# New orders for the opening and for steps 18 to 46, earlier row weights for expert 0, activations moved by 64 bytes, and a last tile in two column halves

## The chip, the core and the metric

The kernel runs as one program on one core of a Trainium2 chip. A core has TensorE (PE, whose weight loads the profile lists apart as PEld), VectorE (DVE), ScalarE (ACT), GpSimd (POOL) and SyncE (SP, which here only issues DMAs). The metric is the device time of one execution in microseconds (us), lower is better.

## The reference, cut to what matters

```python
# attention: 4 batches, 8 heads, 576 positions, 64 wide; banded masks (plain for 4 heads, dilated for 4)
scores = scale * np.matmul(q, k.transpose(0, 1, 3, 2))
scores = np.where(masks, scores, -1e9)
attn = softmax(scores)
x = np.matmul(attn, v)                      # -> 2304 tokens x 512
# dense block, d_ff = 2048
h = x @ w_in
x = (h * np.cos(h)) @ w_out
# 8 experts, two per token, d_ff = 1024
noisy = x @ w_gate + np.log1p(np.exp(x @ w_noise)) * noise
# the two largest of each token, softmax over these two -> weights
for e in range(8):
    out[mask] += top2_w[mask] * (np.maximum(x[mask] @ w1[e], 0.0) @ w2[e])
```

## The kernel before

All large products run as three matmuls each: operands are split into a high and a low part (`PASSES`), hi x hi, hi x lo, lo x hi, in fp32r.

**Opening.** Attention is done in 16 units `u` (four per batch). The string `OPENING` is an order written out by hand: each word is one call, a letter with numbers. S is `a_scores` (scores on PE, maxima on DVE), E `a_exp` (nine exponentials on ACT), N `a_norm` (reciprocal on DVE, then the scaling on POOL, for unit 2 on ACT), T `a_trans` (transposes on PE into one of two PSUM banks, `mid` and `midb`, then a copy by DVE or, with the suffix a, ACT), A `a_av` (values on PE, copies), C `a_shift` (a POOL copy of V), Q and V loads of one unit, W `w_load` (a quarter of the weight block `wm[j]`), B `w_bits` (three DVE instructions that turn the loaded double words into floats), P `w_parts` (high part by ACT, low part by DVE or POOL), X `x_split` (high and low part of the activations) and G a piece of the first product of steps 0 and 1. Every engine takes its part of these calls in this order. `LOADS` is the same for the first DMAs.

**Steps.** The dense block is 72 steps `i`. Steps 0 to 63 take pairs of token blocks; in each, PE does the first product `g1_pair` (12 matmuls 128x512, line 658) and then, for the step two before, the second product `g2_pair` (12 matmuls, line 698, in two halves). `post` makes h*cos(h) of the first product: ACT, DVE, ACT, ACT, DVE, ACT, and a low part by DVE or POOL. Everything else is woven in by the table `BESIDE`: a line `i:pos` says what comes at step `i` at position -1 (after the first product), 0 (after the first half of the second), 1, or 2 (after the second half): weight blocks, the attention of later units (`a_t`, `a_o`, `a_part`, `a_s`, `a_e`, `a_norm`), and the router (`r_rows`, `r_trans`, `r_gate`, `r_logits`, `r_exp`, `r_top`, `r_top2`, `r_pick`, `r_rank`, `r_send`), which ends with indirect DMAs that write a table of tokens for each expert. The set `OTHER` picks a second choice by name: `b..` keeps the bits of `w_bits` in SBUF instead of a PSUM bank, `w..` and `g0_..` give a low part to DVE instead of POOL, `t..` gives a copy of a transpose to DVE instead of ACT, `m..` a copy of values to ACT, `y..` takes the bank `midb`.

**Experts.** After the steps, each expert's tokens are gathered in five tiles. The first product (`s_m`, line 1215; for expert 0 `m_g1`, line 1046) leaves relu(h) as a high and a low part in `hx`; the second product is `m_y` (line 1263): per tile 24 matmuls 128x512, whose stationary operand is a block of 128 columns of `hx` and whose moving operand is a row of the weight tile `w` in another pool. `m_out` scales with the row weights `wts` and sends the tile to the output by an indirect DMA; for the last expert it adds into rows fetched before (DVE, line 1274). The row weights of expert 0 are made by `t_weights(0, 1)`: two tables are loaded, DVE and ACT compute. `q_sum` and `q_split` prepare sums of expert 1's weights on DVE and ACT. After the last tile DVE finds the largest expert, every engine loads that number into a register (`values_load`) and branches over a part for overfull experts.

`hx` lies in a small pool behind `tb` and `wts`, in the order of these three lines:

```python
    tb = c2.tile([P, NE, NTILE, 2], F32, name="tb", bufs=1)
    wts = c2.tile([P, NE * NTILE], F32, name="wts", bufs=1)
    hx = c2.tile([P, WORDS], F32R, name="hx")
```

Of the kernel before, what the change touches and what calls it, by code (L numbers as in the profile page):

```python
# [9 lines left out]
F32 = mybir.dt.float32  # L10
# [8 lines left out]
P = 128  # L19
# [9 lines left out]
NE = 8  # L29
# [25 lines left out]
    "Q0 Q1 Q2 V0 V1 Q3 V2 W00 V3"  # L55
)
OPENING = (
# [49 lines left out]
12:0 w_bits(7,1)
12:1 a_loadv(7) w_parts(7,1) w_piece(7,3)
12:2 a_loadqk(8) w_piece(7,2)
13:-1 w_parts(7,0) a_t(7,0)  # L110
# [9 lines left out]
18:2 a_loadv(8)  # L120
19:0 r_trans(0)
19:1 zero_out(0)
20:0 zero_out(3) a_scores(8)
20:1 a_exp(8) a_loadqk(9)
# [26 lines left out]
30:-1 zero_out(14)
30:0 a_part(11,1)
30:1 r_send(1,0)
31:-1 zero_out(9) x_split(4,0,2) a_part(11,2) x_split(4,2,4) x_split(5,2,4)
31:0 x_split(5,0,2)
31:1 r_send(1,1)
31:2 a_scores(12)
32:-1 a_exp(12)
32:1 a_loadv(12)
32:2 a_loadqk(13)  # L160
33:0 a_scores(13)
33:1 r_rows(2)
33:2 zero_out(12)
34:-1 zero_out(17)
34:0 r_rows(3) r_trans(2)
35:0 a_exp(13)
35:2 r_trans(3)
36:2 a_loadqk(14)
37:2 a_norm(12)
# [1413 lines left out]
```

## Time and profile before

| | us |
|---|---|
| median of 3 runs | 962.65 (962.4 to 963.13) |
| the profiled execution's own time | 964.26 |
| its span, first to last instruction | 962.6 |
| PE busy in it | 936.5 |
| DVE busy | 616.6 |
| ACT busy | 536.0 |
| POOL busy | 398.3 |

The span is in three parts: the opening and first steps (to about 62 us), the steps (to about 520 us) and the experts. A row of the timeline or of the chain says when something began and how long it took; brackets at the end of a timeline row say how long its engine sat idle before it and what ended that.

### The profile page before, as it was taken

Reading aid. Unit: us, or ns where it says so; the run is one execution under the profiler, and the core shown is the slowest. Engines: PE = TensorE matmul, PEld = TensorE weight load, DVE = VectorE, ACT = ScalarE, POOL = GpSimd, SP = SyncE. Lnnn points to the kernel's source line nnn. Section 1 sums busy time; section 2 is a strip of 40 time slices with the busy share of each in tenths; the row PEclk is TensorE's granted clock in tenths of the full one; section 3 lists DMA queues with packets and bytes.
Section 4 is the critical chain, followed back from the end, with each engine's and each line's share of the span. In section 5 each row is a group of like instructions: output and inputs, shape, how many; then the busy total and the mean of one; then the engine's idle time right before and its main releaser. Section 6 shows DMA issues by size and latency. Waiting matters only on the chain.

```text
span 962.6 us, 16062 instructions
## 1 busy us (share of the span) xinstructions
PE 936.5 (97%) x5935; PEld 787.4 (82%) x5935; DVE 616.6 (64%) x1418; ACT 536.0 (56%) x1111; POOL 398.3 (41%) x446
## 2 busy tenths in 40 slices
PE   8799999999999999999999999999999999999997
PEld 5577788777887778888887789889898989888895
DVE  6988884577445753355386775857677695857641
ACT  7867875675565556464574354554555464545530
POOL 6444422334523453234332626253454626263261
PEclk9989999999999999999999999999999999999999
DMA  9852322222330201000243224463534535463521
GB/s 323 289 199 72 98 80 84 72 87 66 82 113 1 72 19 44 1 1 2 80 172 106 40 87 137 110 164 99 140 121 87 173 45 154 110 167 99 127 63 42
DMA packets 52017, 96.95 MB, mean 101 GB/s; under 512 B 12021, under 2 KB 24309, under 8 KB 51936
## 3 DMA queue, kind: packets, MB, share of 16 engines
q1 hardware_dynamic: 42416, 75.68, 23.8%
q0 software_dynamic: 9520, 20.22, 10.1%
q8 instruction: 47, 0.77, 0.4%
q14 instruction: 34, 0.28, 0.1%
HBM read 77.35 MB, written 19.59 MB: 101 GB/s over the span
## 4 chain that ended last, share of the span: by engine, by line
PE 83%; DVE 7%; ACT 4%; DMA 2%; issue 2%; POOL 1%; SPq 0%; POOLq 0%; DVEq 0%; ACTq 0%
PE ye L1263 22%; PE acc L698 16%; PE ph L658 15%; PE pd L1215 5%; PE pa L1215 5%; PE pc L1215 2%; PE pb L1215 2%; PE pk L1215 2%; PE sc L494 2%; PE pe L1046 2%; PE mq L1166 2%; PE mo L582 2%; PE mt L560 1%; PE ph L645 1%; PE mx L726 1%
## 5 line engine op out<-in xcount | busy, mean ns | idle before, releaser
L1263 PE MATMUL ye<-we,hx 128*128 128x512 f32 (+1 forms) x960 | 228.3, 397 | 0.0
L1263 PEld LDWEIGHTS ye<-we,hx 128*128 128x128 f32 (+1 forms) x960 | 174.9, 184 | 44.4
L698 PE MATMUL acc<-wm,g 128*128 128x512 f32 x768 | 198.0, 400 | 3.1 <-ACT wm L347 1.8
L658 PE MATMUL ph<-xhl,wm 128*128 128x512 f32 x768 | 188.4, 393 | 1.0 <-POOL wm L349 0.8
L658 PEld LDWEIGHTS ph<-xhl,wm 128*128 128x128 f32 x768 | 143.5, 189 | 32.6 <-POOL wm L349 1.3
L698 PEld LDWEIGHTS acc<-wm,g 128*128 128x128 f32 x768 | 140.7, 189 | 33.7 <-ACT wm L347 2.2
L675 POOL TENSOR_TENSOR g<-r,g 128x512 fp32r<-128x512 f32 x65 | 83.9, 1291 | 198.7 <-ACT g L673 195.2
L1280 POOL DMA_INDIRECT out<-new,tb x35 | 61.4, 1756 | 177.2 <-ACT new L1277 144.1
L666 DVE SCALAR_TENSOR_TENSOR r<-r,ph 128x512 f32<-128x512 int32 x72 | 49.1, 683 | 66.2 <-ACT r L665 65.8
L670 DVE SCALAR_TENSOR_TENSOR r<-r,ph 128x512 f32<-128x512 f32 x72 | 49.3, 684 | 57.0 <-ACT r L669 56.8
L673 ACT ACTIVATE g<-r 128x512 fp32r<-128x512 f32 x72 | 45.4, 631 | 61.8 <-DVE r L670 41.1
L1127 POOL TENSOR_TENSOR we<-wraw,we 128x512 fp32r<-128x512 f32 x56 | 70.7, 1293 | 17.6 <-ACT we L1126 17.3
L668 ACT ACTIVATE r<-r 128x512 f32<-128x512 f32 x72 | 45.5, 632 | 43.9 <-DVE r L666 43.6
L1112 DVE TENSOR_TENSOR wq<-wraw,wq 128x512 fp32r<-128x512 f32 x98 | 61.7, 686 | 8.9 <-ACT wq L1111 8.2
L665 ACT ACTIVATE r<-ph 128x512 int32<-128x512 f32 x72 | 42.7, 593 | 37.2 <-PE ph L658 31.0
L1111 ACT ACTIVATE wq<-wraw 128x512 fp32r<-128x512 f32 x98 | 54.3, 621 | 12.8 <-DMA wraw<-in_we 8.6
L669 ACT ACTIVATE r<-r 128x512 f32<-128x512 f32 x72 | 45.5, 632 | 2.3
L831 POOL DMA_INDIRECT tab<-pay,si x36 | 36.4, 1012 | 20.6 <-DVE si L824 14.4
L1215 PE MATMUL pd<-xs,wq 128*128 128x304 f32 x224 | 44.4, 302 | 0.0
L1277 ACT ACTIVATE new<-ye,wts 128x512 f32<-128x512 f32 (+1 forms) x30 | 20.6, 686 | 41.8 <-PE ye L1263 41.7
L549 POOL TENSOR_TENSOR s<-s,sm 128x288 f32<-128x288 f32 x42 | 27.9, 692 | 37.7 <-DVE sm L543 31.4
L1222 ACT ACTIVATE hx<-pc 128x304 fp32r<-128x304 f32 x28 | 11.9, 425 | 53.3 <-DVE pc L1235 53.3
(252 smaller groups left out, 1702.8 us busy)
## 6 DMA issues: line engine op xcount, KB each, us to landing
wraw<-in_we SPq DMA_DIRECT2D x64, 512.0 KB, 5.7
raw<-in_wm SPq DMA_DIRECT2D x28, 512.0 KB, 7.7
out<-zt SPq DMA_DIRECT2D x18, 256.0 KB, 4.7
x1d<-x SPq DMA_DIRECT2D x9, 512.0 KB, 2.9
vts<-in_v SPq DMA_DIRECT2D x11, 384.0 KB, 3.9
kts<-in_kT SPq DMA_DIRECT2D x13, 288.0 KB, 3.9
qts<-in_qT SPq DMA_DIRECT2D x13, 288.0 KB, 4.7
piece<-in_wm SPq DMA_DIRECT2D x4, 512.0 KB, 6.1
```

Of the source, the lines that this page charges most:

```text
L658: nc.tensor.matmul(ph, w[:, a, o:o + P], xhl[:, :, x, c, :], start=(c == 0 and n == 0), stop=(c == 3 and n == 2))
L666: nc.vector.scalar_tensor_tensor(r, n, -TWO_PI, ph, op0=ALU.mult, op1=ALU.add)
L668: nc.scalar.activation(r, r, AF.Sin, scale=0.5)
L670: nc.vector.scalar_tensor_tensor(r, r, 0.5, ph, op0=ALU.subtract, op1=ALU.mult)
L675: eng.tensor_tensor(g[:, 1, :], r, g[:, 0, :].bitcast(F32), op=ALU.subtract)
L698: nc.tensor.matmul(ACC[b + t // 2][t % 2], g[:, a, t * P:(t + 1) * P], w[:, x, 1024 + f % 2 * DM:1024 + (f % 2 + 1) * DM], start=(f == 0 a ...
L1111: nc.scalar.activation(w[:, 0, o], src[:, o], AF.Copy)
L1112: eng.tensor_tensor(w[:, 1, o], src[:, o], w[:, 0, o].bitcast(F32), op=ALU.subtract)
L1127: eng.tensor_tensor(t[:, 1, fs], raw, t[:, 0, fs].bitcast(F32), op=ALU.subtract)
L1215: nc.tensor.matmul(b, WQ[e, w][:, wa, o:o + P], XQ[e, x][xa_][j], start=(bank is None and j == 0 and n == 0), stop=(j == 1 and n == 2), sk ...
L1263: nc.tensor.matmul(acc, h[:, a, f, o:o + n], w[:, b, (f % 4) * DM:(f % 4 + 1) * DM], start=(f == 0 and i == 0), stop=(f == 7 and i == 2))
L1280: d = nc.gpsimd.indirect_dma_start(out=out, out_offset=row_of(e, t, n), in_=x, in_offset=None, bounds_check=NT - 1, oob_is_err=False, **how)
```

## The change

`LOADS` takes the first weight quarter before two of the V loads. `OPENING` has the same words in another order, but for X01 and X11, which change engines for their low part (X01 from POOL to DVE, X11 from DVE to POOL). `BESIDE` gets another order at many steps up to 46. `OTHER` loses b41 b43 b71 g0_6 g0_8 m41 t42 t50 w40 w41 w60 y00 y46 and gains g0_15 w53 w70 y12 y45. `wts` gets 16 floats more, of which nothing is used. `t_weights(0, 1)` goes ahead of three `q_sum` of expert 1. The search for the largest expert and the register load go ahead of the last tile's output. The last tile of the last expert computes its 512 columns in two halves.

```diff
-    "Q0 Q1 Q2 V0 V1 Q3 V2 W00 V3"
+    "Q0 Q1 Q2 V0 V1 Q3 W00 V2 V3"
...
-    "C0 S0 W02 S1 E0 N0 E1 W01 S2 T00 N1 E2 S3 T01 C1 E3 T10 W10 T11 N2 C2 T02 C3 N3 A10 T12 A00 B00 "
-    "T20a T21a B01 A01a T22a T30a W20 P00 A20a Q4 X00p X01p A11a A21a W11 X11 W23 V4 S4 W22 W12 P01 W03 "
-    "X10p X21p T32a X20p G10 E4 T31 W21 G00 W13 A30a C4 G11 B11 A31a B10 G01 X31p G12 X30 P10 P11 G02"
+    "S0 S1 E0 W02 N0 S2 E1 W01 C0 E2 T00 T01 N1 S3 W10 E3 N2 C1 T10 T11 C2 C3 T02 A10 N3 T12 A00 B00 "
+    "T20a T21a A01a W20 B01 A11a X01 Q4 T30a V4 T22a P00 A20a W11 W12 X00p X11p A21a W23 P01 X10p W03 "
+    "X21p S4 T32a W13 X20p E4 G10 W22 T31 B10 G00 B11 G01 W21 A30a C4 A31a G02 X31p X30 G11 P10 G12 P11"
...
-0:2 w_parts(0,2) w_load(6,0) a_norm(4)
-1:0 w_load(4,0) w_bits(1,2)
+0:2 a_norm(4) w_parts(0,2)
+1:0 w_bits(1,2)
 1:1 w_parts(0,3) w_parts(1,2)
-2:-1 w_bits(1,3)
-2:0 a_t(4,0) w_bits(2,0) w_load(5,0) w_load(3,3) a_t(4,2) a_t(4,1)
-2:1 a_o(4,0) w_parts(2,0)
-3:-1 w_bits(2,2) w_parts(2,2) w_bits(2,1)
-3:0 w_load(5,1) w_parts(1,3) w_bits(2,3) a_loadqk(5) w_load(4,2) w_parts(2,1)
+1:2 w_load(6,0) w_bits(1,3)
+2:-1 a_t(4,1)
+2:0 a_t(4,0) w_bits(2,0) a_t(4,2) w_load(4,2) w_load(5,0)
+2:1 w_parts(2,0)
+2:2 w_load(3,3)
+3:-1 w_bits(2,2) a_o(4,0) w_bits(2,1) w_parts(2,2) w_load(5,1)
+3:0 w_bits(2,3) a_loadqk(5) w_parts(1,3) w_parts(2,1)
...
-10:0 w_parts(5,3) a_t(6,0)
-10:1 w_parts(5,2) a_o(6,0)
+10:0 a_t(6,0) w_load(6,1) w_parts(5,3)
+10:1 a_loadqk(7) w_parts(5,2)
...
-11:0 a_s(7,0) w_parts(6,1) w_parts(6,2) a_s(7,1)
+11:0 w_parts(6,1) a_o(6,0) w_parts(6,2) a_s(7,0)
...
-24:-1 zero_out(6) a_part(8,2) a_scores(10)
-24:0 a_loadv(9) r_top2(0) zero_out(4) a_part(9,0)
...
-25:2 r_top(1) a_part(9,1) a_exp(10)
-26:-1 a_loadqk(11) r_rank(0)
...
+25:-1 a_scores(10)
+25:0 a_part(9,0)
+25:1 a_exp(10)
+25:2 a_part(9,1) r_top(1)
+26:-1 a_loadqk(11) r_rank(0) r_send(0,0) zero_out(7)
 26:0 a_part(9,2) a_norm(10)
...
-28:1 r_send(0,0) r_rank(1)
...
+28:0 a_loadv(10) r_rank(1)
...
-        for f in fs:
-            w = WE[e, 2 + f // 4]
-            for i, (a, b) in enumerate(PASSES):
-                nc.tensor.matmul(acc, h[:, a, f, o:o + n], w[:, b, (f % 4) * DM:(f % 4 + 1) * DM],
-                                 start=(f == 0 and i == 0), stop=(f == 7 and i == 2))
+        for c0, c1_ in parts(e, t):
+            for f in fs:
+                w = WE[e, 2 + f // 4]
+                for i, (a, b) in enumerate(PASSES):
+                    nc.tensor.matmul(acc[:, c0:c1_], h[:, a, f, o:o + n],
+                                     w[:, b, (f % 4) * DM + c0:(f % 4) * DM + c1_],
+                                     start=(f == 0 and i == 0), stop=(f == 7 and i == 2))
+
+    def parts(e, t):
+        return ((0, DM // 2), (DM // 2, DM)) if (e, t) == (NE - 1, NTILE - 1) else ((0, DM),)
...
-            nc.vector.scalar_tensor_tensor(x, acc, w, x, op0=ALU.mult, op1=ALU.add)
+            for c0, c1_ in parts(e, t):
+                nc.vector.scalar_tensor_tensor(x[:, c0:c1_], acc[:, c0:c1_], w, x[:, c0:c1_], op0=ALU.mult, op1=ALU.add)
...
-    wts = c2.tile([P, NE * NTILE], F32, name="wts", bufs=1)
+    wts = c2.tile([P, NE * NTILE + 16], F32, name="wts", bufs=1)[:, :NE * NTILE]
...
     q_split(1, "A22")
+    t_weights(0, 1)
     q_sum(1, "S1")
...
-    t_weights(0, 1)
     for t in range(2):
         m_out(0, t)
...
+                if t == NTILE - 1:
+                    over = nc.values_load(nti[0:1, 0:1], min_val=0, max_val=NT)
                 m_out(e, t)
...
-    over = nc.values_load(nti[0:1, 0:1], min_val=0, max_val=NT)
```

## Rows read from the trace of the kernel before

**Rows 1.** The page: busy time by engine, and granted clock in 40 slices
```profile
PE 936.5 (97%) x5935; PEld 787.4 (82%) x5935; DVE 616.6 (64%) x1418; ACT 536.0 (56%) x1111; POOL 398.3 (41%) x446
PEclk9989999999999999999999999999999999999999
```
**Rows 2.** Windows: length, busy us (instructions) PE PEld DVE ACT POOL, clock, DMA
```profile
30.00:35.00 5.00, 5.00 (x55) 3.61 (x53) 4.75 (x8) 4.55 (x20) 3.11 (x4) 1.00 0.99 343
...
38.00:48.00 10.00, 4.31 (x20) 2.70 (x19) 9.60 (x17) 6.67 (x13) 3.20 (x4) 0.99 0.64 232
48.00:54.60 6.60, 6.03 (x33) 4.67 (x32) 6.33 (x12) 3.36 (x7) 1.85 (x2) 0.50 0.81 301
...
553.00:556.40 3.40, 3.40 (x11) 2.43 (x10) 1.96 (x9) 1.17 (x4) 1.58 (x3) 0.51 0.68 192
```
**Rows 3.** Timeline of the opening: start us, us, engine, line, operands [idle before]
```profile
16.12 1.30 SPq L317 DMA_DIRECT2D raw<-in_wm  x2
...
18.66 0.95 DVE L542 TENSOR_SCALAR sm<-sm 128x9 f32<-128x9 f32 x1
...
19.95 2.50 ACT L546 ACTIVATE ahead<-ahead,sm 128x96 f32<-128x96 f32 x9 [0.60 <-DVE sm L543]
...
23.16 0.60 SPq L299 DMA_DIRECT2D vts<-in_v  x1
...
30.14 0.68 DVE L339 TENSOR_SCALAR bits<-raw 128x512 uint32<-128x512 uint32 x1
```
**Rows 4.** Timeline of steps 2 and 3, all engines
```profile
45.68 0.51 PE L560 MATMUL mt<-ident,s 128*96 128x128 f32 x3 [1.06 <-DVE cut L341]
...
47.18 0.47 ACT L563 ACTIVATE at<-mt 96x384 f32<-96x384 f32 x1
...
47.71 0.85 PE L560 MATMUL mt<-ident,s 128*96 128x128 f32 x3 [1.52 <-ACT at L563]
...
49.13 1.29 PE L582 MATMUL mo<-at,vts 96*64 96x64 f32 x20 [0.57 <-ACT at L563]
...
50.35 2.93 PE L698 MATMUL acc<-wm,g 128*128 128x512 f32 x6
...
51.92 0.55 DVE L565 COPY at<-mt 96x384 f32<-96x384 f32 x1
```
**Rows 5.** Timeline of steps 10 and 25 to 26, PE and DVE
```profile
108.08 0.78 PE L582 MATMUL mo<-at,vts 96*64 96x64 f32 x20 [0.65 <-DVE at L565]
...
214.42 2.41 DVE L771 SCALAR_TENSOR_TENSOR po<-po,s 128x16 f32<-128x16 f32 x7
...
217.25 0.17 PE L810 MATMUL mr<-os,tri 128*128 128x8 bf16 x1 [1.22 <-DVE xraw L590]
```
**Rows 6.** Timeline while expert 0's last tiles are gathered
```profile
542.32 5.94 POOL L1009 DMA_INDIRECT xg<-x1d,tb  x1 [6.12 <-DMA tb<-tab]
...
551.95 0.69 DVE L1027 TENSOR_TENSOR xa<-mgx,xa 128x512 fp32r<-128x512 f32 x1 [4.61 <-ACT xa L1026]
```
**Rows 7.** Chain that ended last: start us, us, engine, tile, line, instructions
```profile
150.02 2.72 PE ph L658 x12
...
459.13 2.76 PE ph L645 x24
...
606.63 5.60 PE ye L1263 x24
...
613.50 5.50 PE ye L1263 x24
...
620.27 16.61 PE ye L1263 x72
...
928.85 28.01 PE ye L1263 x120
```
**Rows 8.** Timeline: a DVE instruction on 256 columns, and the last output
```profile
558.17 0.42 DVE L1058 SCALAR_TENSOR_TENSOR hx<-pe,hx 128x256 fp32r<-128x256 f32 x1 [2.46 <-ACT hx L1049]
...
956.89 0.75 DVE L1274 SCALAR_TENSOR_TENSOR old<-ye,wts,old 96x512 f32<-96x512 f32 x1 [4.85 <-PE ye L1263]
```

More of the change, by code (lines that the diff above doesn't have):

```diff
@@ L107 @@
[L107 to L110, printed above, removed]
+12:-1 w_bits(6,3) w_bits(7,0) a_norm(7) w_parts(6,3) w_piece(7,3)
+12:0 a_loadv(7) w_bits(7,1)
+12:1 w_parts(7,1)
+12:2 w_parts(7,0) w_piece(7,2)
 13:0 w_bits(7,2) a_t(7,1)
-13:1 w_bits(7,3)
+13:1 a_t(7,0) w_bits(7,3)
+13:2 a_loadqk(8)
 14:-1 w_parts(7,2)
-14:0 zero_out(5) a_t(7,2)
+14:0 a_t(7,2)
+14:1 zero_out(5)
 15:-1 x_split(3,0,2)
-15:0 a_o(7,1) x_split(2,0,2) a_o(7,0) x_split(2,2,3,1) x_split(3,2,4) x_split(2,3,4,1)
+15:0 x_split(2,0,2) a_o(7,1) a_o(7,0) x_split(2,2,3,1) x_split(3,2,4) x_split(2,3,4,1)
@@ L117 @@
 16:0 w_parts(7,3)
-17:2 r_rows(0)
+17:0 r_rows(0)
 18:0 r_rows(1) r_trans(1)
[L120 to L124, printed above, removed]
+19:1 r_trans(0) zero_out(0)
+19:2 zero_out(3)
+20:0 a_scores(8)
+20:1 a_exp(8)
+20:2 a_loadqk(9)
 21:0 r_gate(0)
 21:1 a_scores(9)
-21:2 zero_out(2)
 22:-1 r_gate(1) r_logits(0) r_exp(0)
-22:0 a_norm(8)
-22:1 a_exp(9) r_top(0) a_norm(9)
-22:2 a_loadqk(10)
+22:0 a_loadv(8) a_norm(8)
+22:1 r_top(0) a_exp(9) a_norm(9)
@@ L140 @@
 26:0 a_part(9,2) a_norm(10)
-26:2 zero_out(1) a_scores(11)
-27:-1 r_top2(1) a_part(10,0)
-27:1 zero_out(7)
+26:2 a_scores(11)
+27:-1 a_part(10,0) zero_out(1)
+27:0 r_top2(1)
+27:1 zero_out(10) zero_out(14)
 27:2 r_pick(1)
-28:-1 a_loadqk(12)
-28:0 a_loadv(10) zero_out(10)
-28:1 r_send(0,0) r_rank(1)
-29:-1 a_exp(11) a_norm(11) a_part(10,1)
-29:0 a_part(10,2) r_send(0,1) zero_out(11) a_loadv(11)
-29:2 a_part(11,0)
[L151 to L160, printed above, removed]
+28:0 a_loadv(10) r_rank(1)
+28:1 a_loadqk(12)
+29:-1 r_send(0,1) a_exp(11) a_norm(11) a_part(10,1)
+29:0 a_part(10,2)
+29:1 a_loadv(11)
+29:2 a_part(11,0)
+30:-1 zero_out(11)
+30:0 r_send(1,0)
+30:1 r_send(1,1)
+30:2 a_part(11,1)
+31:-1 zero_out(9) x_split(5,0,2) x_split(4,0,2) a_part(11,2) x_split(5,2,4) x_split(4,2,4)
+31:2 a_scores(12) a_loadqk(13)
+32:0 zero_out(17)
+33:-1 a_exp(12)
@@ L161 @@
 33:0 a_scores(13)
 33:1 r_rows(2)
[L163 to L169, printed above, removed]
-38:-1 r_gate(2)
-38:1 r_logits(2) zero_out(15)
-38:2 r_exp(2)
+34:0 a_loadv(12) r_rows(3) r_trans(2)
+35:0 zero_out(12)
+35:2 r_trans(3) a_exp(13)
+37:1 a_loadqk(14)
+38:-1 r_gate(2) zero_out(15)
+38:0 a_norm(12)
+38:2 r_logits(2) r_exp(2)
 39:-1 a_part(12,0)
-39:0 r_gate(3) r_top(2) zero_out(16)
+39:0 r_top(2) r_gate(3) zero_out(16)
@@ L177 @@
 40:0 a_part(12,2) a_scores(14)
-40:2 a_loadv(13) a_norm(13)
-41:0 r_logits(3)
-41:1 a_part(13,0) r_exp(3) a_loadqk(15)
-41:2 r_rank(2) a_part(13,1) r_send(2,0) a_part(13,2) zero_out(13)
-42:-1 a_exp(14) a_norm(14) r_top(3)
+40:1 a_norm(13)
+41:-1 a_loadv(13)
+41:0 zero_out(13) r_logits(3)
+41:1 a_part(13,0) a_loadqk(15) r_exp(3)
+41:2 r_rank(2) a_part(13,1)
+42:-1 a_exp(14) a_norm(14) a_part(13,2) r_top(3)
 42:0 a_part(14,0)
-42:2 a_loadv(14) r_top2(3) a_scores(15)
-43:0 r_pick(3) a_part(14,1)
-43:1 a_exp(15)
+42:1 a_loadv(14)
+42:2 a_scores(15)
+43:0 r_top2(3) a_exp(15) r_pick(3)
+43:2 r_send(2,0)
 44:-1 r_rank(3)
-44:1 a_norm(15)
+44:0 a_norm(15)
+44:1 a_part(14,1)
 45:-1 r_send(3,0) a_part(14,2)
@@ L239 @@
 """
-OTHER = set("b00 b01 b02 b03 b13 b20 b30 b31 b33 b41 b42 b43 b51 b62 b63 b71 b72 e4 e7 g0_0 g0_1 g0_12 g0_14 g0_4 g0_6 g0_8 m40 m41 m50 m51 m60 m61 m70 m71 n2 t42 t50 t60 t71 w00 w02 w10 w12 w40 w41 w50 w60 w61 w63 w71 w72 y00 y01 y02 y10 y21 y30 y32 y42 y46 y50 y54 y55 y66 y70 y73 y75".split())
+OTHER = set("b00 b01 b02 b03 b13 b20 b30 b31 b33 b42 b51 b62 b63 b72 e4 e7 g0_0 g0_1 g0_12 g0_14 g0_15 g0_4 m40 m50 m51 m60 m61 m70 m71 n2 t60 t71 w00 w02 w10 w12 w50 w53 w61 w63 w70 w71 w72 y01 y02 y10 y12 y21 y30 y32 y42 y45 y50 y54 y55 y66 y70 y73 y75".split())
 @with_exitstack
@@ L1440 @@
     t_weights(1, NE)
+    mxc = small.tile([P, 2], F32, tag="mxc", name="mxc", bufs=1)
+    nc.vector.tensor_reduce(mxc[:, 0:1], cnt, axis=AX.X, op=ALU.max)
+    nti = small.tile([P, 2], I32, tag="nti", name="nti", bufs=1)
+    nc.vector.tensor_scalar(mxc[:, 1:2], mxc[:, 0:1], float(CAP), None, op0=ALU.max)
+    nc.vector.tensor_scalar(mxc[:, 1:2], mxc[:, 1:2], 1.0 / P, (63.5 - CAP) / P + NTILE, op0=ALU.mult, op1=ALU.add)
+    nc.vector.tensor_copy(nti, mxc)
     for k in range(4):
```

53 lines of the change are left out of this document (25 added, 28 removed).

## The prediction, made before the changed kernel was run

> **What bounds the kernel now.** I read the page first: PE is busy 936.5 us of a span of 962.6, 97%, and the slices of the granted clock show two places under 9 tenths' steady level [rows 1]. So the span is PE's own work plus some 26 us in which it stands still, plus stretches in which it works at the lower clock. The windows say where: from 38 to 48 us PE works 4.31 us of 10 while DVE works 9.60, and from 48 to 54.6 PE is busy but at a granted clock of 0.50, the 1.2 GHz level; a second stretch at 0.51 follows the wait for expert 0's last tokens, near 553 [rows 2]. In the first 60 us DVE is therefore the bound and PE's clock falls after the standstill; after that PE's work is the bound, and single waits of PE add to it. The timelines were read for these waits, and the chain that ended last for the pace of the matmuls. What can be gained is the standstill near 40 us, the waits, the tail, and the pace itself.
>
> The profiled execution took 964.26 us, 1.6 over the median of the runs, 962.65. I work with differences and take them off the median.
>
> **The change part by part.**
>
> *Opening up to 36 us.* The reciprocal for unit 2 goes ahead of two copies on DVE. Before, ACT stood idle 0.60 us for it, and on DVE its first instruction alone took 0.95, under a POOL copy [rows 3]. PE is without idle time from 30 on [rows 2], so 0.60 less there moves all that follows: -0.6. V4 now stands ahead of W11, W23 and the rest on SP's queue. It went out at 23.16, when the last reader of the first V was done, W11 at 16.12 [rows 3]. So these quarters start some 7 us later than before; the first of them is needed by the bits of block 1 at 30.14 [rows 3], which leaves over 6 us from issue to use. I cost it at nothing; if that cover were gone, DVE, the bound here, would wait for the DMA and everything behind it. X01 and X11 swap DVE and POOL for one piece each: nothing.
>
> *Steps 2 and 3.* Three waits of PE are in the timeline: 1.06 for a bank held by weight bits, 1.52 and 0.57 for copies of transposes by ACT [rows 4]. The 1.52 arises because the first transpose of unit 4 is copied at 47.18, behind the first ACT instruction of step 2's `post`, and the next one needs its bank. Now `a_t(4,1)` comes at 2:-1, with its copy ahead of that instruction; `t42` leaves OTHER, so DVE loses a copy of 0.55 [rows 4]; `a_o(4,0)` goes one step later, its work is not saved. As DVE is the bound here (9.60 of 10, 6.33 of 6.60 [rows 2]), what counts is DVE's time: 0.55, and with the 0.60 from above the weights of step 4 are ready 1.15 earlier. I take -1.2 for the opening and steps 0 to 4 together. At best the three waits all go, -3.15; at worst PE, which now has `a_t(4,1)` ahead of the first half of `g2_pair`, waits for POOL's scaling there: another wait like the 1.06, less the 0.60: +0.5.
>
> *Steps 5 to 17.* At step 10 PE waits 0.65 for DVE's copy of a transpose before `a_o(6,0)` [rows 5]; that call moves to 11:0, over a first product (2.72 us [rows 7]) later: -0.65. w40, w41, w60, g0_6 and g0_8 go from DVE to POOL, which is 41% busy against DVE's 64% [rows 1]: nothing, as no wait of PE stands on them. Moved loads of weights only change their order on SP, long ahead of use: nothing.
>
> *Steps 18 to 46.* At step 26 `r_rank(0)` holds PE for 1.22, because its bank waits for a copy of values that DVE makes only after `r_top(1)`, whose seven long instructions alone take 2.41 [rows 5]. The new order has `a_part(9,1)` ahead of `r_top(1)`: -1.2. `a_scores(10)` and `a_exp(10)` come closer together, so ACT waits for POOL there; behind that on ACT is the high part of step 25, wanted two steps (over 10 us of PE) later: nothing. `r_send(0,0)` now stands on POOL's queue directly behind `r_rank(0)` and in front of `a_norm(10)`; the transposes that need that scaling are a step away: nothing. For waits of the new order that I don't see I put +0.4, an estimate between nothing and the 0.65 and 1.22 of the two waits above [rows 5]; ends 0 and +1.2.
>
> *Expert 0's row weights.* `t_weights(0, 1)` now makes DVE wait for the tables, and three `q_sum` and the low parts behind them wait with it. The tables were there at 542.32, where POOL's wait of 6.12 for them ends, and DVE was idle for 4.61 before 551.95 [rows 6]. Nine small instructions at 2.41/7 = 0.34 [rows 5] are 3.1, which leaves 1.5 for the wait. `m_out` of expert 0 comes earlier, but nobody on PE waits for it: nothing. If the cover is gone, the low part of the transposed tokens comes late.
>
> *Tail.* The last tile's addition took 0.75 on 512 columns, and 0.42 is the row for 256 [rows 8]; the first half now runs beside PE: -0.33. 48 matmuls of 256 columns instead of 24 of 512: 2.76/24 = 115 ns against 28.01/120 = 233 [rows 7], 5.52 against 5.60: -0.08. The search for the largest expert and the register load leave the end, where they lay beside the output's DMA: nothing. Together -0.4; ends 0 and -0.6.
>
> *Activations moved by 64 bytes.* While PE streams a row of `w` it loads the next block of `hx`; the distance between the two in SBUF changes by 64 bytes for all 960 matmuls of `m_y`. The trace shows that one shape at one clock has several paces: 2.72/12 = 226.7 ns in the steps, 5.50/24 = 229.2, 16.61/72 = 230.7, 5.60/24 = 233.3 and 28.01/120 = 233.4 in `m_y` [rows 7]. In the last expert nothing else of weight runs beside them, so it isn't other engines' work. One expert of the middle six has 5.60 + 5.50 + 16.61 = 27.71; six of these, 28.01 and expert 0 at 120 x 230.7 make 222.0 us, 231.2 ns each. At the pace of the steps it would be 217.6, -4.4; at the slowest pace seen here 224.1, +2.1. No row shows the new distance, and I take the middle, -1.1.
> The Trainium skill speaks against any effect here: SBUF — State Buffer, "Who interferes with whom", gives PE two independent read ports, one for the moving operand and one for weight loads, and says that PE waits on nobody. By it this term is 0 and the sum 1.1 us less of a gain. That two paces stand in one kernel for one shape [rows 7] fits it badly, but shows no cause.
>
> Sum: -1.2 - 0.65 - 1.2 + 0.4 - 0.4 - 1.1 = -4.15; off the median, 958.5 us.
>
> **The rivals.**
> *The distance does nothing.* -3.05: 959.6. For it: places with different distances differ by under 3%; against: 229.2 and 233.4 for the same instructions.
> *PE's gains are not kept.* What PE gains in the opening and at the two waits is lost again at the next place where DVE is the bound, as it has 9.60 of 10 us from 38 to 48 [rows 2], or in new waits of the same size. Left are the tail and a part of the rest: about -0.8, 961.9. Against it: after 62 us PE has hardly a wait over 0.2.
> *The new distance is the worse one.* If the pace rises by one more step of the kind seen, 233.4 - 229.2 = 4.2 ns, to 237.6, `m_y` takes 228.1, +6.1; with -3.05 from the rest it ends at +3.05, 965.7. It makes the kernel slower from 1.9 + 3.05 = 4.95 us, 5.2 ns each, a pace above 236.4. For it: no row says on which side the new place lies.
> *The slow stretch goes.* If the waits of steps 2 and 3 become short enough that the clock doesn't fall, 6.03 us of PE's work at 0.50 [rows 2] take half: -3.0 more, 955.5. Against: even without the three waits PE stands still for some 3 us from 38 to 48. The stretch near 553 can also come out longer or go, by 3.40/2 = 1.7 us either way, as it is set off by a wait.
>
> **How the numbers follow.** What a measurement of this kernel can tell from no change is about 0.2%, 1.9 us: faster is below 960.7, slower above 964.6. Forecast 0.38, distance does nothing 0.22, slow stretch goes 0.09: all faster, 0.69. Gains not kept 0.18: within. Worse distance 0.13: slower. The range goes from 954.8, the forecast with the best distance (-3.3) or the best opening (-2), or the rival without the slow stretch, to 963.4, gains not kept and a longer stretch near 553 (+1.7). Left out are most of the worse distance and the corners, under 0.2.
>
> **What would show it.** Right: PE's busy share from 38 to 48 rises and step 4's first product (after 60 us before) starts about 1.2 earlier; no wait of PE before `a_o(6,0)` and before `r_rank(0)`; the chain's last piece on `ye` is followed by a DVE instruction of about 0.42; `m_y` at about 230 ns. Wrong: pieces of `ye` of 5.7 us or more per 24; a new wait of PE over 0.5 us between 60 and 310; the low part at 551.95 late and PE waiting behind it; PE idle after 30 us for weights whose load stood behind V4.

## The result, and the profile after

The changed kernel takes 949.63 us (median, 948.66 to 950.09) against 962.52 of the kernel before: a ratio of 0.9864, 95% interval 0.9846 to 0.9881, some 13 us less. The forecast was 958.5, its range 954.8 to 963.4. The sign was right, the size a third of what came. The profiled execution of the changed kernel took 948.66, its span is 947.0.

The page first, busy time by engine and the granted clock in 40 slices, to be read beside [rows 1].

```profile
PE 928.2 (98%) x5959; PEld 785.4 (83%) x5959; DVE 607.5 (64%) x1416; ACT 536.6 (57%) x1112; POOL 409.0 (43%) x448
PEclk9999999999999999999999999999999999999999
```

The span less PE's busy time was 962.6 - 936.5 = 26.1 us and is 947.0 - 928.2 = 18.8. So 7.3 us came from standing still less, and 8.3 from less busy time for the same work, that is from a faster pace or less time at the lower clock. The prediction had put most of its gain on the first kind.

The windows of the opening follow (length, busy us and instructions of PE, PEld, DVE, ACT, POOL, then clock and DMA), first of the changed kernel.

```profile
38.00:42.00 4.00, 0.00 (x0) 0.00 (x0) 3.93 (x8) 1.73 (x4) 0.97 (x2) 1.00 0.92 335
42.00:45.60 3.60, 2.90 (x9) 2.32 (x9) 3.43 (x6) 3.19 (x6) 2.56 (x4) 0.53 0.97 358
...
48.00:54.60 6.60, 6.60 (x63) 5.07 (x62) 6.29 (x11) 4.07 (x9) 3.03 (x3) 1.00 1.05 400
```

PE's timeline there (start, length, instruction, and in brackets the idle time before it with what ended it), first two waits of the kernel before that stand ahead of those in [rows 4], then the changed kernel:

```profile
41.05 0.50 PE L698 MATMUL acc<-wm,g 128*128 128x512 f32 x1 [1.79 <-ACT wm L347]
42.86 1.43 PE L698 MATMUL acc<-wm,g 128*128 128x512 f32 x5 [1.31 <-DVE wm L349]
```

```profile
42.70 0.88 PE L565 MATMUL mt<-ident,s 128*96 128x128 f32 x3 [4.80 <-POOL s L554]
...
58.22 1.19 PE L663 MATMUL ph<-xhl,wm 128*128 128x512 f32 x4 [0.63 <-POOL wm L354]
```

PE now waits once, 4.80 us, for POOL's scaling ahead of `a_t(4,1)`, where before it had these two waits and the three of [rows 4] among little pieces of work; then it is busy without a gap until a wait of 0.63. Together that is 5.43 us of waits against 6.25, so PE stands still hardly less; what shrank more is the stretch at 0.5 (1.2 GHz). It comes earlier and lasts some 3.4 us, against 6.8 (the window of [rows 2] holds 6.6 of them). DVE is as busy as before: 3.93 of 4.00.

The place that mattered most is where expert 0's last tiles are gathered, at [rows 6] before. The kernel before around that gather, in which DVE runs its sums beside it, the next gather follows, and PE waits twice:

```profile
541.24 3.70 DVE L1105 TENSOR_TENSOR wraw<-wraw 128x512 f32<-128x512 f32 x6
...
544.85 2.49 DVE L1112 TENSOR_TENSOR wq<-wraw,wq 128x512 fp32r<-128x512 f32 x4
...
548.57 1.02 POOL L1009 DMA_INDIRECT xg<-x1d,tb  x1 [0.31 <-issue]
...
550.63 0.66 PE L1024 MATMUL mgx<-ident,xg 128*128 128x128 f32 x4 [1.67 <-DMA xg<-x1d,tb]
...
552.02 0.66 PE L1024 MATMUL mgx<-ident,xg 128*128 128x128 f32 x4 [0.74 <-DMA xg<-x1d,tb]
```

All engines of the changed kernel:

```profile
534.56 0.17 DVE L995 SCALAR_TENSOR_TENSOR we__5531<-tb 128x5 f32<-128x5 f32 x1 [1.17 <-DMA tb<-tab]
...
534.92 1.05 POOL L1014 DMA_INDIRECT xg<-x1d,tb  x1 [6.64 <-DMA tb<-tab]
...
536.03 3.69 DVE L1110 TENSOR_TENSOR wraw<-wraw 128x512 f32<-128x512 f32 x6
536.27 1.33 POOL L1014 DMA_INDIRECT xg<-x1d,tb  x1 [0.31 <-issue]
...
540.76 1.03 PE L1029 MATMUL mgx<-ident,xg 128*128 128x128 f32 x8
...
542.05 1.28 DVE L1032 TENSOR_TENSOR xa<-mgx,xa 128x512 fp32r<-128x512 f32 x2
```

The gather takes 1.05 us where [rows 6] has 5.94, and PE's transposes on 540.76 wait for nothing. In the kernel before they waited 1.67 and 0.74 and the clock fell to 0.51 for 3.4 us behind that [rows 2].

Stage by stage, from the starts of the same matmuls in the two profiled executions: 3.7 us are won by step 6, 1.6 more by step 12, 0.4 by step 18, 2.2 by step 46, 4.5 at expert 0's gather, 2.8 in the rest of the experts (nearly all in `m_y`), and 0.4 behind the last matmul. These are 15.6; the medians say 13, since the profiled execution of the kernel before lay 1.6 us over the median of its runs and that of the changed kernel 1.0 under. The first stage is the one that depends most on the execution: against a second one of the kernel before (below) only 1.8 us are won by step 6.

### The profile page after: what moved, and what is told of

Read it like the earlier page. It is cut to its first block, busy times and chain, and to the rows that moved or that the text cites. A ratio compares the mean times of both kernels' runs of the same rounds, so it can differ in the third digit from the quotient of the medians.

```text
span 947.0 us, 16105 instructions
## 1 busy us (share of the span) xinstructions
PE 928.2 (98%) x5959; PEld 785.4 (83%) x5959; DVE 607.5 (64%) x1416; ACT 536.6 (57%) x1112; POOL 409.0 (43%) x448
## 5 line engine op out<-in xcount | busy, mean ns | idle before, releaser
L1269 PE MATMUL ye<-we,hx 128*128 128x512 f32 (+2 forms) x984 | 224.0, 386 | 0.0
L1291 POOL DMA_INDIRECT out<-new,tb x35 | 73.0, 2086 | 160.9 <-ACT new L1288 131.4
L1142 POOL DMA_INDIRECT xg<-x1d,tb x35 | 37.0, 1057 | 15.3 <-issue 10.6
```

Source lines behind the costliest of these rows:

```text
L1269: nc.tensor.matmul(acc[:, c0:c1_], h[:, a, f, o:o + n], w[:, b, (f % 4) * DM + c0:(f % 4) * DM + c1_], start=(f == 0 and i == 0), stop=(f ...
L1291: d = nc.gpsimd.indirect_dma_start(out=out, out_offset=row_of(e, t, n), in_=x, in_offset=None, bounds_check=NT - 1, oob_is_err=False, **how)
```

## Experiments

Times are compared with the kernel before on the same chip, as a ratio with its 95% interval; in microseconds that is the ratio's distance from 1, times about 962.

**The activations' place alone.**

```diff
-wts = c2.tile([P, NE * NTILE], ...)
+wts = c2.tile([P, NE * NTILE + 16], ...)[:, :NE * NTILE]
```

> The kernel before with the activations moved by 64 bytes and nothing else. Theory, the pace of m_y depends on where hx lies: 24 matmuls of the last expert come 226.7 ns apart instead of 233.3, and the other tiles are faster too, as in the changed kernel, where the time of m_y from its tile 3 of expert 0 to the end shrank by 2.8 us; so 2.8 us less than before, about 959.7. Rival, the pace came from the new orders (other things running beside PE, another clock): the pace stays at 229 to 233 ns and the time within 0.5 us of before.

Ratio 0.9970 (0.9958 to 0.9981), so -2.9 us (-4.0 to -1.8). The pieces of `ye` have the changed kernel's pace; here one piece of 24 of the changed kernel, and of this one:

```profile
700.66 5.63 PE L1269 MATMUL ye<-we,hx 128*128 128x512 f32 x24
```

```profile
711.80 5.63 PE L1263 MATMUL ye<-we,hx 128*128 128x512 f32 x24
```

A merged row holds one matmul's own 0.39 us at its end, so (5.63 - 0.39)/23 = 227.8 ns from start to start. The theory holds; the orders have no part in the pace.

**The row weights alone, and the wait alone.** First `t_weights(0, 1)` moved as in the change; then left in its old place, with one small instruction on DVE that reads the same tables.

```diff
 q_split(1, "A22")
+t_weights(0, 1)
 q_sum(1, "S1")
...
 m_y(0, 2, range(EARLY_F, MID_F))
-t_weights(0, 1)
```

```diff
 q_split(1, "A22")
+hold = small.tile([P, NTILE], F32, tag="hold", name="hold", bufs=1)
+nc.vector.tensor_scalar(hold, tb[:, 0, :, 1], 0.0, None, op0=ALU.add)
 q_sum(1, "S1")
```

> The kernel before with t_weights(0, 1) moved ahead of the three q_sum and nothing else. Theory, DVE keeps POOL from its gather: in the kernel before POOL's first gather for expert 0's tile 3 took 5.94 us beside ten long DVE instructions, in the changed kernel 1.05, because DVE then waits for the same tables; so the gather takes about 1 us, PE's waits of 1.67 and 0.74 before the transposes go, and so does the stretch at the lower clock (3.40 us at half the clock, 1.7): 4.1 us less than before, 958.4. Rival, the slow gather of the kernel before was an accident of one execution, or came from another order: within 0.5 us of before.

> The kernel before with t_weights(0, 1) in its old place, and one added small DVE instruction ahead of the three q_sum that reads the tables of expert 0, so that DVE waits for them; its output is not used. Theory, what counts is that DVE is held until POOL's gather can start: the gather takes about 1 us and the time falls like that of weights_alone, by about 4 us. Rival, what counts is that the row weights are ready earlier: the gather stays at about 6 us and the time stays within 0.5 us of before.

Ratios 0.9958 (0.9941 to 0.9975), so -4.0 us, and 0.9968 (0.9955 to 0.9980), so -3.1. POOL's first gather with the row weights early:

```profile
541.80 1.05 POOL L1009 DMA_INDIRECT xg<-x1d,tb  x1 [5.71 <-DMA tb<-tab]
```

and DVE and POOL with the wait alone, DVE first:

```profile
541.71 0.17 DVE L1407 TENSOR_SCALAR hold<-tb 128x5 f32<-128x5 f32 x1 [0.70 <-DMA tb<-tab]
541.81 3.70 DVE L1105 TENSOR_TENSOR wraw<-wraw 128x512 f32<-128x512 f32 x6
...
541.99 1.44 POOL L1009 DMA_INDIRECT xg<-x1d,tb  x1 [6.17 <-DMA tb<-tab]
```

Both take the long gather away. So it isn't that the weights are ready earlier, but that DVE stands until the tables are there, so that its run isn't long under way when POOL's gather comes. How far ahead DVE may be is not shown: with the wait alone its first sum began 0.18 us before the gather, and the gather ended 0.93 behind the end of this one sum (541.99 + 1.44 against 541.81 + 0.69):

```profile
541.81 0.69 DVE L1105 TENSOR_TENSOR wraw<-wraw 128x512 f32<-128x512 f32 x1
```

The second is not a clean measure of the price: the added tile moved everything behind it by 32 bytes, and the last expert's pace went from 233.3 to 228.8 ns. Over all of `m_y` the matmuls came 231.2 ns apart before and 230.1 with the wait alone, so some 0.9 us of its 3.1 are an effect of the place.

**The kernel before a second time, and the row weights put back.**

```diff
 q_split(1, "A22")
-t_weights(0, 1)
...
 m_y(0, 2, range(EARLY_F, MID_F))
+t_weights(0, 1)
```

> The kernel before, unchanged, looked at a second time, since its first profiled execution was 1.6 us over the median of its runs. If the slow gather near 542 us and the long stretch at the lower clock near 48 us belong to the kernel, both are here again, the gather with 5 us or more and the stretch with about 6.8 us; if they were accidents of that execution, the gather takes about 1 us and the span is 4 us shorter than the first.

> The changed kernel with t_weights(0, 1) at its old place. Theory, the six long sums of DVE then run while POOL starts its first gather, which takes about 6 us instead of 1.05, PE waits for it and its clock falls to half for some 3.4 us: 4.0 to 4.5 us more than the changed kernel, some 953.8. Rival, the new orders ahead of it have moved the two engines against each other so that they no longer meet: within 0.5 us of the changed kernel.

The kernel before took 963.43 in this execution, span 961.7. The changed kernel with the weights back takes 953.42, a ratio of 0.9908 (0.9892 to 0.9925) where the changed kernel has 0.9864: some 4.2 us more. Both have the long gather. DVE, POOL and PE of the kernel before, second execution:

```profile
539.05 3.69 DVE L1105 TENSOR_TENSOR wraw<-wraw 128x512 f32<-128x512 f32 x6
540.15 5.92 POOL L1009 DMA_INDIRECT xg<-x1d,tb  x1 [5.94 <-DMA tb<-tab]
...
542.67 2.49 DVE L1112 TENSOR_TENSOR wq<-wraw,wq 128x512 fp32r<-128x512 f32 x4
...
548.59 0.66 PE L1024 MATMUL mgx<-ident,xg 128*128 128x128 f32 x4 [1.81 <-DMA xg<-x1d,tb]
```

and POOL, DVE and PE of the changed kernel with the weights back:

```profile
535.40 5.75 POOL L1014 DMA_INDIRECT xg<-x1d,tb  x1 [6.31 <-DMA tb<-tab]
...
534.12 3.69 DVE L1110 TENSOR_TENSOR wraw<-wraw 128x512 f32<-128x512 f32 x6
537.74 2.49 DVE L1117 TENSOR_TENSOR wq<-wraw,wq 128x512 fp32r<-128x512 f32 x4
...
543.51 0.66 PE L1029 MATMUL mgx<-ident,xg 128*128 128x128 f32 x4 [1.77 <-DMA xg<-x1d,tb]
```

DVE's ten instructions, each with both inputs in SBUF, end at 542.67 + 2.49 = 545.16 in the first; the gather ends at 540.15 + 5.92 = 546.07, 0.92 later. In the second it is 540.23 and 541.15, 0.92 again; and in [rows 6] the gather's end, 542.32 + 5.94, is 0.92 behind 547.34, the end of the same ten (544.85 + 2.49 above). All eleven traces with the long gather have this 0.92, although the gather began at different places in DVE's run. So it does its work when DVE's run is over, and needs some 0.92 to 1.05 for itself.

**The opening, the middle, and both.** The order of the named steps from the changed kernel, with the engine choices that belong to them, in the kernel before.

```diff
-LOADS, OPENING and steps 0 to 3 of BESIDE of the kernel before
+those of the changed kernel
-OTHER: t42 m41 y00 y46
+OTHER: y12 y45
```

```diff
-steps 4 to 17 of BESIDE of the kernel before
+those of the changed kernel
-OTHER: b41 b43 b71 g0_6 g0_8 t50 w40 w41 w60
+OTHER: g0_15 w53 w70
```

> The kernel before with the new order of loads, of the opening and of steps 0 to 3, with the engine choices that belong to them (t42, m41, y00, y46 out, y12 and y45 in); from step 4 on all as before. Theory, from the two traces: step 6 starts 3.7 us earlier, and the granted clock is at 0.5 for about 3.4 us instead of 6.8: 3.7 us less than before, 958.8. Rival, what the opening gains is lost again at the old order of steps 4 to 17, where DVE is late: less than 1.5 us less.

> The kernel before with the new order of steps 4 to 17 and the engine choices that belong to it (b41, b43, b71, g0_6, g0_8, t50, w40, w41, w60 out, g0_15, w53 and w70 in). Theory, from the two traces: the changed kernel won 1.6 us from step 8 to 12 and 0.4 to step 18, so 2.0 us less than before, 960.3. Rival, that gain needs the opening's earlier weights, and alone only the wait of 0.65 at step 10 goes: 961.6.

> The kernel before with the new order of loads, opening and steps 0 to 17 together (opening_alone and middle_alone in one). Theory, the middle's gain needs the opening's: in the changed kernel no wait took the place of the two that went at steps 9 and 10, in middle_alone DVE waited 2.43 us for a weight piece and PE 1.12 behind it; together they give 1.7 of the opening and 1.7 of the middle, 3.4 us less than before. Rival, the wait for the weight piece comes here too: 1.7 to 2.3 us less.

The opening gives a ratio of 0.9982 (0.9972 to 0.9992), -1.7 us. The middle gives 0.9990 (0.9979 to 1.0001), -1.0, not told apart from nothing. Both together give 0.9955 (0.9939 to 0.9972), -4.3 (-5.9 to -2.7), by the middle value more than the two added; the intervals don't exclude the plain sum.

In the middle alone PE's two waits at step 10 are gone, 1.6 us by step 12 against the kernel before's second execution, and 1.3 of it is lost again at step 14. DVE and PE there, and the same DVE instruction in the changed kernel:

```profile
130.50 0.43 DVE L340 TENSOR_SCALAR cut<-piece 128x512 uint32<-128x512 uint32 x1 [2.43 <-DMA piece<-in_wm]
...
132.99 0.51 PE L561 MATMUL mt<-ident,s 128*96 128x128 f32 x3 [1.11 <-DVE at L566]
```

```profile
126.94 0.43 DVE L344 TENSOR_SCALAR cut<-piece 128x512 uint32<-128x512 uint32 x1 [0.91 <-DMA piece<-in_wm]
```

The load of this weight piece took 5.6 us from issue to landing in the first and 4.1 in the second; DVE waits for it, the copy of a transpose stands behind that on DVE, and PE waits for the copy. With the opening's order DVE waited 0.71 and PE not at all. So this is a wait that takes the place of the one removed, and whether it comes hangs on a transfer's length; why that was longer is open.

A second part of the gap is the clock behind expert 0's gather. With opening and middle together the gather still took 5.82 and PE waited 1.71 and 0.69, but the clock stayed up (window as above, last of it clock and DMA); below it the kernel before, second execution:

```profile
544.00:551.00 7.00, 6.04 (x41) 5.14 (x41) 2.73 (x11) 3.04 (x7) 4.26 (x6) 1.00 0.62 181
```

```profile
548.00:555.00 7.00, 5.86 (x26) 4.45 (x27) 2.43 (x10) 2.67 (x5) 4.52 (x6) 0.76 0.62 184
```

So the same two waits cost 1.7 us more or not, as the clock falls behind them or doesn't: of the eleven traces with the long gather it fell in seven. I can't say from these runs what decides it.

**Steps 18 to 46.**

```diff
-steps 18 to 46 of BESIDE of the kernel before
+those of the changed kernel
```

> The kernel before with the new order of steps 18 to 46 and nothing else. Theory, from the changed kernel's trace against the second look at the kernel before: PE's wait of 1.22 before r_rank(0) goes, and smaller waits near steps 25, 42 and 44 shrink, 2.2 us between step 18 and step 46, and all of it is kept: 2.2 us less than before. Rival, as in middle_alone a new wait takes the place of the old one when the earlier steps keep their order: within 0.5 us of before.

Ratio 0.9986 (0.9977 to 0.9996), -1.3 us (-2.2 to -0.4). The wait of 1.22 is gone; in this kernel and in the changed one, `r_rank(0)`:

```profile
214.62 0.18 PE L812 MATMUL mr<-os,tri 128*128 128x8 bf16 x1
```

```profile
209.93 0.18 PE L815 MATMUL mr<-os,tri 128*128 128x8 bf16 x1
```

Its trace has 2.2 us less between step 18 and step 46 than the kernel before's second execution. The interval holds the theory's -2.2 and the rival's -0.5 alike: that the wait goes is shown by the trace, how much of it is kept is not settled by the times.

**Where the activations may lie.** Each expert gets a place of its own (in words of 4 bytes): in one kernel 32 bytes more from expert to expert; in another the same with everything behind one small tile, weights and activations, moved by 32 bytes besides; in a third places around 256 bytes further on.

```diff
-HG[e] = hx[:, H0:H0 + 2 * NE * 640]...
+HG[e] = hx[:, H0 + 8 * e:H0 + 8 * e + 2 * NE * 640]...
```

```diff
-mxc = small.tile([P, 2], ...)
+mxc = small.tile([P, 2 + 13], ...)[:, :2]
```

```diff
-HG[e] = hx[:, H0:H0 + 2 * NE * 640]...
+D = (0, 68, 72, 76, 80, 84, 96, 144)
+HG[e] = hx[:, H0 + D[e]:H0 + D[e] + 2 * NE * 640]...
```

> The kernel before, with the activations of expert e (1 to 7) moved by 32 e bytes from their place, the weights where they were. Expert 2 then has the place of the changed kernel, expert 0 that of before. Theory, the pace of m_y depends on the place of hx: expert 2 has 227 to 228 ns as in the changed kernel, expert 1 and the odd ones may be slow, and some pattern with a period appears over the seven. Rival, only the move as a whole matters (what else lies where): all seven keep 229 to 233 ns.

> As sweep_hx, and everything in SBUF behind one small tile, weights and activations alike, moved by another 32 bytes. Theory, what counts is the distance between the streamed weights and the activations: each expert has the pace that it has in sweep_hx. Rival, what counts is where each of the two lies by itself: experts of the same distance have another pace here, and hold_alone, in which both had moved by 32 bytes and the last expert had 228.8 instead of 233.3 ns, speaks for this.

> The kernel before, with the activations of experts 1 to 7 moved by 272, 288, 304, 320, 336, 384 and 576 bytes. In sweep_hx only the move by 64 bytes was fast; there the distance between a streamed row of weights and the block of activations loaded beside it is 256 bytes more than a multiple of 512. Theory, what is fast is a distance that is a multiple of 256 bytes: expert 4 (320, distance a multiple of 512) and expert 7 (576, as 64) have 226 to 228 ns in their tiles of 128 rows, the other five 229 to 234. Rival, a multiple of 512 away from the changed kernel's place only: expert 7 alone is fast. Rival, 64 bytes was fast for another reason: neither is.

From start to start, in ns, second tile of each expert (128 rows; one gap of some 0.31 us, in which PE transposes the next expert's tokens, is left out) and last tile (96 rows); the place is given as the move from the kernel before. The first column is the kernel before itself:

| moved by, bytes | 0 | 32 | 64 | 96 | 128 | 160 | 192 | 224 |
|---|---|---|---|---|---|---|---|---|
| 128 rows | 229.4 | 233.5 | 227.8 | 233.4 | 233.4 | 233.9 | 232.3 | 233.1 |
| 96 rows | 233.5 | 226.7 | 230.0 | 228.9 | 228.3 | 230.9 | 231.6 | 231.0 |

| moved by, bytes | 272 | 288 | 304 | 320 | 336 | 384 | 576 |
|---|---|---|---|---|---|---|---|
| 128 rows | 231.6 | 233.1 | 228.4 | 227.8 | 226.6 | 233.5 | 226.7 |
| 96 rows | 228.9 | 226.7 | 231.0 | 230.0 | 226.7 | 228.3 | 230.0 |

The first tiles of experts 1, 2 and 3 in the first of the three kernels, 32, 64 and 96 bytes:

```profile
605.25 5.76 PE L1263 MATMUL ye<-we,hx 128*128 128x512 f32 x24
...
659.44 5.63 PE L1263 MATMUL ye<-we,hx 128*128 128x512 f32 x24
...
712.82 5.77 PE L1263 MATMUL ye<-we,hx 128*128 128x512 f32 x24
```

and experts 4 and 6 in the third, 320 and 384 bytes:

```profile
765.17 5.63 PE L1263 MATMUL ye<-we,hx 128*128 128x512 f32 x24
...
871.74 5.76 PE L1263 MATMUL ye<-we,hx 128*128 128x512 f32 x24
```

Places 256 bytes apart have the same pace (32 and 288, 64 and 320, 128 and 384). The fast ones at 64, 320 and 576 lie 256 bytes apart. I read from the compiled programs that there the distance from the streamed weights is a multiple of 256 bytes; the traces have no addresses, so the runs themselves show the period and not its zero. 304 and 336, 16 bytes to either side of 320, are fast too, the latter in every tile. With everything moved by 32 bytes besides, each expert's second tile keeps its pace within 1 ns (232.9, 227.1, 233.2, 233.3, 234.3, 232.4, 233.1 from 32 to 224), and so do the tiles of 96 rows but for one (226.7 instead of 231.6 at 192): the distance counts. It doesn't tell all: at a move of 0 two paces stand in one kernel, 229 and 233.3, and the 32 bytes of the wait-alone kernel, which left the distance as it was, changed one into the other for the last expert. Why a distance should matter no run shows.

**The changed kernel again, and versions that might beat it.**

```diff
-OTHER = set("... g0_4 ...")
+OTHER = set("... g0_4 g8_6 g8_7 ...")
```

```diff
-H0, H1 = 56, 56 + 2 * NE * 384
+H0, H1 = 60, 60 + 2 * NE * 384
```

> The changed kernel, with the low parts of the activations of the last two steps (g8_6 and g8_7) made on DVE instead of POOL. In the changed kernel POOL takes 1.27 us for each, PE waits 0.56 and 0.62 for them near 503 and 507 us, and DVE stands idle for 0.64 and 1.28 just there; DVE's instruction of this shape takes 0.69. Theory: both waits go, 1.1 us less than the changed kernel, about 948.5. Rival, DVE's next instruction on the same chain is put off by 0.7 each and PE waits for that: no gain.

> The changed kernel with the low parts of its last two steps on DVE, beside the changed kernel on the same chip. In its first look the waits of 0.56 and 0.62 were gone and one of 0.68 for ACT had come; so theory: 0.5 us less than the changed kernel. Rival: no difference that can be told.

> The changed kernel, unchanged, a second time. Theory, the time that the opening saves at the lower clock belongs to the new order: the stretch at 0.5 near 42 us is again 3.4 us long, or at most 6.8, and the clock of nearly all its executions is over 0.995, where those of the kernel before have 0.991 to 0.996. Rival, the short stretch was luck of one execution: the clocks scatter like those of before, and the time is 951 to 953.

> The changed kernel with the activations moved by another 16 bytes, 80 in all, the distance to the weights then 272 bytes more than a multiple of 512. In sweep_far the expert at 336 bytes, 16 more than the fast place at 320, had 226.7 ns in all its tiles, the last one of 96 rows too, which has 230.0 in the changed kernel. Theory, the rule of the distance holds here too: all tiles of experts 1 to 7 have 226.7, some 733 x 0.7 + 157 x 3.3 ns = 1.0 us less than the changed kernel, about 948.0 to 948.6. Rival, a start that is not a multiple of 32 bytes slows ACT and DVE, which write the activations: no gain, or a loss.

> Both additions together: the activations moved by 80 bytes and the low parts of the last two steps on DVE. Theory: 1.0 and 0.5 us less than the changed kernel, about 947.5. Rival: the two gains can't be told from noise, 949.

The changed kernel comes out at the same ratio, 0.9864 (0.9847 to 0.9880), 948.91 us. The granted clock over its span was 0.996 to 0.997 in these four executions, 0.995 to 0.998 in the first four; the kernel before has 0.991 to 0.996.

With the low parts on DVE the ratio was 0.9861 and 0.9857 (0.9841 to 0.9881, 0.9840 to 0.9873). The changed kernel's two waits, and the one that took their place:

```profile
504.12 2.60 PE L690 MATMUL acc<-wm,g 128*128 128x512 f32 x10 [0.56 <-POOL g L680]
...
508.09 2.11 PE L690 MATMUL acc<-wm,g 128*128 128x512 f32 x8 [0.62 <-POOL spacer L835]
```

```profile
507.57 1.69 PE L690 MATMUL acc<-wm,g 128*128 128x512 f32 x5 [0.68 <-ACT g L678]
```

0.56 + 0.62 - 0.68 = 0.5 us by the trace, and no difference that the times can tell.

With another 16 bytes all tiles of experts 1 to 7 ran at 226.6 to 226.9 ns, as expected, but most of those of expert 0 at 233, and some matmuls of 304 columns were slower, the commonest kind 142.4 ns from start to start against 140.0. The kernel before took 966.73 on that chip and has no trace from there, so chip and place can't be told apart. Ratios 0.9862 (0.9846 to 0.9879) and, with the low parts, 0.9853 (0.9835 to 0.9870): not told apart from the changed kernel's 0.9864. I call neither better.

## Why the prediction was wrong

The parts taken alone add up to the whole: opening and middle -4.3, steps 18 to 46 -1.3, row weights -4.0, place -2.9, tail -0.35 by the trace, together -12.85; measured, 962.5 x 0.0136 = -13.1. So the sum was wrong by its terms, not by a term left out of it. The agreement is no close test: each part has an interval of some 1 to 1.7 us to either side, and as the clock behind the gather stayed up in the trace with opening and middle together, up to 1.7 us may stand in the sum twice.

*Expert 0's row weights: forecast nothing, measured -4.0. This is the step that failed.* It asked whether the wait of DVE for the tables would hurt what stands behind it on DVE, and answered that 4.61 us of idle time cover it. They just did: in the changed kernel DVE goes from its sums straight to the low part, at 542.05, and PE waits for nothing there. It didn't ask whom DVE's instructions were holding. The row for it stood in [rows 6]: the first gather there took 5.94 us, and the next of the same kind, at 548.57, took 1.02. I read that row only for the time at which the tables were there. PE's two waits for this gather, 1.67 and 0.74, stand in no term; the clock of 0.51 behind them [rows 2] stands in the prediction only as 1.7 us by which the end may scatter, not as something that this part of the change could take away. Had the 5.94 been compared with its neighbours and with what DVE did meanwhile, its price could have been estimated: about 5 us of gather, of which PE felt 2.4, and 1.7 of clock.

The Trainium skill, SBUF — State Buffer, "Who interferes with whom", has a rule for it: a DVE instruction with two SBUF inputs contends with a GpSimd instruction that reads SBUF, and whichever comes second is kept out until the first is done. The gather that ends 0.92 us behind DVE's last instruction agrees with that (it reads its row numbers from SBUF). It differs in that the long gather was kept out not for one instruction but for the rest of an unbroken run, nine instructions in [rows 6]. Gathers that follow at once on another, as those at 536.27 to 541.50 us of the changed kernel, run beside the same sums in 1.3 to 1.5 us, and each ends 0.87 to 0.89 behind the end of a single sum, as the rule has it. What lets these through after one instruction and not the other no run here shows.

*Activations moved by 64 bytes: forecast -1.1, measured -2.9; mechanism right, size off.* The term named the distance as the cause, and the paces of [rows 7] as the bounds, -4.4 to +2.1; the result lies between them. Taking the middle was the error of size: the paces are not spread evenly, one kind of place gives 226.6 to 227.8 ns for tiles of 128 rows and nearly all others 231.6 to 234.3. The rival in which the distance does nothing falls; the one with a worse distance was possible, as most other places are slow, but none of them reached its 237.6 ns: the slowest here has 234.3. PE's two read ports, which the Trainium skill on the same page calls independent, would have given 0; the runs contradict that 0, with 226.7 against 233.5 ns for one shape at one clock. Whether the two ports are what meets there no run shows.

*Opening, steps 0 to 4: forecast -1.2, measured -1.7 (-2.7 to -0.8) alone.* The size is right, the way only partly, so that it came near is in part luck. The worst case of this term, that PE waits for POOL's scaling ahead of `a_t(4,1)`, came true: not as another 1.06 but as 4.80, and it cost nothing, as the five older waits went for it. DVE, as said, stayed the bound, and the changed kernel pays 0.63 for a weight's low part at step 4, a new wait. The sign was step 4 some 1.2 us earlier; it starts 5.0 earlier than in the first execution of the kernel before, and 3.7 of that are left at step 6. What I gave 0.09, the slow stretch going, came by half: in the nine traces with the new opening it lasts 3.4 us in five and 6.8 in four, in the ten with the old one 6.8 to 13.7 in all.

*Step 10: forecast -0.65, measured -1.0 (-2.0 to +0.1) alone.* PE's wait before `a_o(6,0)` is gone as forecast, and so is one of 0.84 for a weight's low part on POOL in the first product of the same step, which I hadn't costed. Alone, most of it was lost again behind a weight piece; with the opening it was kept. The prediction's remark that PE has hardly a wait over 0.2 after 62 us was a misreading: the trace has 14, 10.3 us together.

*Steps 18 to 46: forecast -1.2 + 0.4, measured -1.3 (-2.2 to -0.4).* Right: the wait before `r_rank(0)` is gone. Whether the +0.4 for unseen waits was needed the interval doesn't tell; the trace, with 2.2 us less, shows no need of it.

*Tail: forecast -0.4, in the trace -0.35; the amount right, the reason wrong.* The span goes on 5.36 us behind PE's last matmul, 5.71 before. But DVE's two half additions are one row behind it, where the kernel before has the whole one of [rows 8]:

```profile
938.76 2.83 PE L1269 MATMUL ye<-we,hx 128*96 128x256 f32 x23
...
941.63 0.87 DVE L1285 SCALAR_TENSOR_TENSOR old<-ye,wts,old 96x256 f32<-96x256 f32 x2 [4.82 <-PE ye L1269]
942.78 0.93 POOL L1291 DMA_INDIRECT out<-old,tb  x1 [4.64 <-POOLq L1510]
```

PE's last matmul ends at 941.59. The first half waited for it as well, so nothing ran beside PE, and two halves take 0.87 where one whole took 0.75. The output's DMA goes out 1.19 us behind PE, 1.07 before: 0.12 lost. The gain, 0.47, lies behind that DMA's start (4.17 us to the end, 4.64 before), where the search for the largest expert and the register's load were, which I had costed at nothing. Why this end is shorter was not taken apart. The 0.08 for matmuls of 256 columns didn't come either: they run 116.2 ns apart, 232.4 for two, where whole ones at the same place have 230.0.

*The range.* Its low end, 954.8, is a little under what its own terms give (958.5 - 3.3 = 955.2 for the best distance). It took in the best distance or the best opening, but no bound at all for the row weights, whose price was set at nothing with a cover and not from both sides. With that term from -4.1 (the two waits, 2.4, and the clock, 1.7) to 0 the range would have reached 950.7, close to the time that came. One reading beside it was wrong without harm: the slices of [rows 1] show one place under 9, not two; the second low stretch stands in [rows 2] alone.

## What to carry to other kernels

When one instruction's row shows several times the duration of its neighbours of the same kind, find out what runs on the other engines between its start and its end before you cost a change there, and look at its end: a gather that ends a fixed time behind the end of another engine's run was probably kept out by that run, and holding that engine back for a moment tests it. A wait that is added to an engine can pay, if it keeps the engine's long run from being under way when another engine's short instruction on the critical path comes.

The pace of matmuls that stand back to back is worth a look by tile: where one shape has several paces at one clock, try the operands at several places by a multiple of 16 or 32 bytes, in one kernel, before believing in any of them.

## What the runs showed that I had not expected

- POOL's first gather for expert 0 took 5.7 to 6.4 us in every kernel in which DVE didn't wait for the tables (the kernel before and nine others here) and ended 0.92 behind the last of DVE's ten two-input instructions each time; it took 1.04 to 1.44 where DVE was held for the tables (the changed kernel, the row weights alone, the wait alone, and the versions with the low parts on DVE or 16 bytes more).
- The pace of `m_y` repeats every 256 bytes of distance between streamed and loaded operand: the places 64, 320 and 576 give 226.7 to 227.8 ns per matmul of 512 columns in the tiles of 128 rows, others up to 234; 16 bytes more gives 226.7 for the tiles of 96 rows as well.
- One order of the opening has stretches at the lower clock of very different length from one execution to the next: one of 6.8 us in the first of the kernel before [rows 2], two of some 3.4 in its second, and 13.7 in the kernel with the row weights alone, whose opening is the same (over 11 of these 13 us):

```profile
40.00:53.00 13.00, 9.53 (x42) 6.92 (x43) 12.66 (x22) 7.84 (x17) 3.98 (x5) 0.56 0.80 291
```

The kernel before scattered from 960.3 to 963.7 us on the chip of that run. How much of it is due to these stretches was not measured; with DVE the bound there, the time that they cost PE is in part hidden.
